# Handing out expert slots after the third, fifth and last group of tokens instead of after every group

## The chip, the cores and the metric

The kernel runs on one core of a Trainium2 chip. The metric is the device time of one execution in microseconds, the median of several runs. A verdict calls a change faster or slower if it moves the time by more than 2%.

## What is computed

A recurrent attention layer is followed by a mixture of experts that sends each token to one expert.

```python
# attention: batch B = 4, heads H = 8, S = 768 steps, head size D = 40, all float32
for t in range(S):
    y[:, :, t] = einsum('bhd,bhde->bhe', r_t, state)
    Sa = einsum('bhde,bhe->bhd', state, a_t)
    state = state * w_t[:, :, None, :] - einsum('bhd,bhe->bhde', Sa, b_t) + einsum('bhd,bhe->bhde', v_t, k_t)
# mixture of experts: N = 3072 tokens of 320, E = 8 experts, F = 1024, capacity N // E * 2
x = y.transpose(0, 2, 1, 3).reshape(B * S, H * D)
logits = x @ w_gate
expert_idx = argmax(logits, axis=1)
gate_w = softmax(logits)[token, expert_idx]
for i in range(N):                       # slots are handed out in the order of the tokens
    e = expert_idx[i]
    if counts[e] < capacity:
        disp[e, counts[e]] = x[i]; pos[i] = counts[e]; counts[e] += 1; keep[i] = True
y = relu(disp @ w1) @ w2
out[i] = gate_w[i] * y[expert_idx[i], pos[i]]        # where keep[i]
```

A token's slot within its expert is the number of earlier tokens that chose the same expert. So slots can be handed out in pieces, if each piece adds the counts of those before it.

## The kernel before

**The scan.** The 768 steps are cut into six groups of 128 (numbers 0 to 5), each group into two chunks of 64. The 32 pairs of batch and head are held in two halves (pr 0 and 1). Within a group the recurrence is solved in a closed form; the state passes from chunk to chunk. For each group there are these steps, told with their lines:

- Decay on VectorE (DVE): products of w by two scans, L378 and L388, with small steps between (L382 to L401, which give the factors wf), and products with them, L458 and L462.
- Matrices on TensorE (PE), L479, one for each half and chunk. ScalarE (ACT) copies them out: X (L66) and the parts of xd and x21 (L61, L503). GpSimd (POOL) masks X (L69).
- The inverse on DVE: a transpose (L578), 62 small elimination operations (L592 and L594 in turn, each needs the one before), two transposes back (L599, L603). Its tiles xd, x21, xu and nu exist once, so that the next group's matrices may overwrite them only when this group is done with them. PE combines the result in blocks of 32 (L623), with copies on ACT between (nt, x, nu; L57, L61).
- The chain, for each half and chunk: decay of the state ST on POOL (L672), products with the state and with X on PE (L693, L697), a copy zv and the sum zs on DVE (L710), a product with the inverse (L721), copies sat and sv, a transpose (L743), copies u, and the new state (L756 on PE, L765 on DVE).
- The output for each half and chunk: qp (L775 on PE, copied and masked, L66, L69 or L72), two products on PE (L791, L794), and y (L805 on DVE). ACT and POOL turn y into an x16 tile in float16 (L57, L856, L857), SyncE (SP) sends it through a DMA transpose (L862) to xT, and PE multiplies that with the gate's weights (L873) to logits, which ACT copies to lg (L878). A group gives four such tiles of 128 tokens, 24 in all.

**Slots.** route, called for each group, has five steps. first (L1110 to L1115, and four additions L1141) finds each token's expert and sums the one-hot rows of the tiles on DVE. count (L1147 to L1149) counts with three matmuls. place (L1155 to L1160) adds the counts of the earlier groups (base) and gives slots. gate (L1120 on ACT, L1121 to L1123 on DVE) gives the weight. Then one scatter for each tile (L1126), an indirect DMA issued by POOL, writes the token's number and weight to the slot's place in one of four tables meta in DRAM (tile number modulo four, so that a scatter waits for the landing of that four tiles before it).

**The experts.** The first 384 slots of experts 0 and 1 can be filled from the first five groups alone in most cases. An early expert uses them while the last group is still under way: it loads slot rows (emm), gathers x rows by POOL, transposes them by DMAs from SP (L944), and multiplies (L960, L1293). It needs the route of group 4. After the scan the experts run one after the other (L1420, L1293), with weights that are scaled on ACT (L1212) and DVE (L1213).

**What sets the order.** The code doesn't state an order within the scan. Each step is given to a list scheduler (Schedule.order) with the engine and the time it is thought to take ("V1.9" is 1.9 us on DVE, "A1.25|V.72" leaves a choice between ACT and DVE), with what it needs, and with which buffers it takes and frees. The scheduler has a clock for each engine and picks, again and again, the step with the lowest score: its start, plus an offset by kind of step and engine (LATER), plus MU times a planned time, minus O_TAIL times the length of what follows it. PRICE weighs the engines where a step may go to several. So a number in these tables can change the order on all engines, and which engine does a copy. The tiles of each kind are counted in BUFS. Each engine then runs its own instructions strictly in that order.

Of the kernel before, what the change touches and what calls it, by code (L numbers as in the profile page):

```python
# [232 lines left out]
def scan_part(ctx, tc, two, w, kb, a, r, vt, v, wg, xd, lg, ident, up, SX, slot2, route, prefetch, fill, early):  # L233
# [23 lines left out]
    LATER = {"R": -5.787, "chain": -0.017, "chain:A": 0.307, "chain:P": -0.014, "chain:V": -0.256,  # L257
             "comb": -0.007, "comb:A": 0.394, "comb:P": 0.904, "decay": 1.569, "decay:V": 0.357,
             "diag": -0.034, "diag:A": 0.978, "early": -2.453, "early:G": 0.469, "early:L": 1.687,
             "early_h": 1.778, "early_h:A": -4.479, "early_h:P": -0.724, "early_h:V": -6.743,  # L260
             "early_o": -0.047, "early_o:A": -0.427, "early_o:G": -3.502, "early_x": -3.485,
             "early_x:G": 0.908, "early_x:S": 3.21, "et": -0.621, "et:A": 1.197, "et:P": 0.131, "fill": 4.274,
             "fill:G": -0.037, "gate": 0.055, "gate:G": -0.339, "gate:P": 0.26, "gate:S": -0.32,
             "gate_store": 2.098, "gate_store:L": -3.063, "inverse": 0.815, "kt": 0.567, "kt:P": -0.305,
             "load_a": 1.14, "load_a:L": -1.165, "load_kb": -0.86, "load_kb:L": -2.23, "load_r": 5.886,
             "load_r:L": 0.968, "load_u": 0.991, "load_u:L": 3.288, "load_vt": 0.808, "load_vt:L": -1.101,
             "load_w": -2.214, "load_w:L": -5.588, "mula": 0.698, "mula:V": 0.924, "mulk": -0.886,
             "mulk:V": 1.741, "out": 0.102, "out:P": -0.049, "out:V": -0.009, "prefetch": 0.015,
             "prefetch:A": 0.642, "prefetch:L": -0.989, "prefetch:V": 1.544, "route": 0.842, "route:A": -14.34,
             "route:G": -3.654, "route:P": 0.544, "route:V": 0.373, "sat": -16.107, "state": -0.132,  # L270
             "state:P": 0.475, "unit": 0.317, "unit:A": -1.263, "xd": -8.639, "xt": -1.178, "xt:A": 0.367,
             "xt:P": -0.155, "xt:V": 0.135}
# [747 lines left out]
def tile_kernel(ctx, tc, w, kb, a, r, vt, v, w_gate, w1, w2, out, capacity):  # L1020
# [109 lines left out]
    def route(i, s_):  # L1130


        tiles = slice(B * i, B * i + B)
# [16 lines left out]

        def place():
            ps = s_["ps"]
            rank = glob.tile([P, B, E], F32, name="rank")
            slot = glob.tile([P, B], F32, name="slot")
            nc.vector.tensor_add(rank, ps[:, 0:B * E].rearrange("p (t e) -> p t e", e=E),  # L1155
                                 base[:, i:i + 1, :].to_broadcast([P, B, E]))
            nc.vector.tensor_add(base[:, i + 1, :], ps[:, B * E:(B + 1) * E], base[:, i, :])
# [3 lines left out]
            if EARLY and i == NI - 2:  # L1161
                nc.vector.tensor_sub(most_a, base[0:1, i + 1, 0:2], ebase[0:1, 0:2])
                nc.vector.tensor_scalar_add(base[:, i + 1, 0:2], ebase[:, 0:2], float(CS - EB))

        return first, count, place, lambda: gate(glob, s_["d"], B, tiles), lambda bi: scatter(B * i + bi)
# [442 lines left out]
```

## Time and profile before

| what | us |
|---|---|
| median of 3 runs (713.77 to 723.05) | 720.71 |
| the profiled execution | 720.66 |
| its span in the profile | 718.7 |
| busy in the span: PE / DVE / ACT / POOL | 532.4 / 450.5 / 348.8 / 282.2 |

The profile is of one execution. Busy times are sums over the whole span; the kernel has a scan, up to about 500 us, and the experts behind it, with different limits, so a stretch is read by itself. In rows of the timeline the first number is the start in us, the second the length in us, then engine, line, operation, output and input, and, in brackets, the idle time of the engine before it with what ended it. "x4" stands for four instructions taken together. In rows of groups a bar parts busy time and mean length in ns from the idle time before.

### The profile page before, as it was taken

The page shows a single profiled execution, that of the slowest core. Times are in us where ns is not written, and L with a number is a line of the kernel's source. Part 1 is how long each engine was busy: PE and PEld are TensorE (multiplying, and loading weights), DVE is VectorE, ACT ScalarE, POOL GpSimd, SP SyncE. Part 2 cuts the span into 40 slices and gives each one's busy share as a digit, 9 for nine tenths or more (in the row PEclk, how much of TensorE's full clock was granted, in tenths as well). Part 3 has the DMA queues.
Part 4 walks back from the last instruction along what each step waited for, and adds up shares of the span by engine and source line. Part 5 has one row for each costly group of instructions (what it writes and reads, how often), then busy time and mean ns, then how long its engine had stood idle before and what let it go on. Part 6 is the DMA issues. An engine that isn't in the chain of part 4 may idle for free. (4 is left out here: it accounts for less than half of the span.)

```text
span 718.7 us, 25037 instructions
## 1 busy us (share of the span) xinstructions
PE 532.4 (74%) x10804; PEld 416.3 (58%) x10804; DVE 450.5 (63%) x871; ACT 348.8 (49%) x751; POOL 282.2 (39%) x380
## 2 busy tenths in 40 slices
PE   1712877768776878587589577585988999999891
PEld 0612766757665767577578476453663655665560
DVE  7999688889688888777748953054433254345120
ACT  4613853675467556654476464334444255245120
POOL 4600454075409541854065325404252153343411
PEclk9965799669857995897579959698998999999996
DMA  8970096917661785276425536746859757856400
GB/s 312 302 231 1 27 206 176 268 46 218 189 214 19 219 218 189 42 201 191 147 52 123 148 105 121 140 104 181 219 103 240 186 110 188 196 152 189 111 20 13
DMA packets 106362, 109.87 MB, mean 153 GB/s; under 512 B 70745, under 2 KB 88667, under 8 KB 106241
## 3 DMA queue, kind: packets, MB, share of 16 engines
q1 hardware_dynamic: 97968, 92.34, 49.1%
q0 software_dynamic: 4256, 9.99, 5.0%
q10 hardware_dynamic: 4016, 5.83, 3.0%
q8 instruction: 87, 1.43, 0.8%
q14 instruction: 35, 0.28, 0.1%
HBM read 83.60 MB, written 10.94 MB: 132 GB/s over the span
## 5 line engine op out<-in xcount | busy, mean ns | idle before, releaser
L1430 DVE SCALAR_TENSOR_TENSOR hh<-ps,hh 128x480 f16<-128x480 f32 (+2 forms) x72 | 37.0, 559 | 107.3 <-ACT hh L1427 107.3
L1293 PE MATMUL ps<-w,hh 128*128 128x320 f16 (+1 forms) x672 | 92.7, 299 | 0.0
L1420 PE MATMUL ps<-xT,w 128*128 128x480 f16 (+1 forms) x448 | 85.4, 354 | 5.9 <-DMA xT<-xt 5.9
L1126 POOL DMA_INDIRECT meta<-mt,sloti x24 | 41.7, 1739 | 114.4 <-DVE se L382 72.9
L1293 PEld LDWEIGHTS <-hh 128*128 128x128 f16 (+1 forms) x696 | 71.1, 103 | 24.3 <-issue 1.6
L594 DVE TENSOR_TENSOR nu<-nu,xd 128x31 f32<-128x31 f32 (+15 forms) x186 | 80.2, 431 | 5.6
L592 DVE TENSOR_TENSOR xd<-xu,nu 128x31 f32<-128x31 f32 (+15 forms) x186 | 79.3, 426 | 5.6
L1420 PEld LDWEIGHTS <-w 128*128 128x128 f16 (+1 forms) x512 | 43.7, 99 | 66.9 <-issue 28.0
L69 POOL TENSOR_SCALAR_AFFINE_SELECT qp<-qp 64x512 f32<-64x512 f32 x86 | 59.7, 694 | 42.2 <-ACT qp L66 30.4
L69 POOL TENSOR_SCALAR_AFFINE_SELECT X<-X 64x512 f32<-64x512 f32 x48 | 45.9, 956 | 65.7 <-ACT X L66 56.9
L1297 POOL DMA_INDIRECT out_dram<-ob,ri x26 | 26.9, 1036 | 106.8 <-ACT ob L1446 33.7
L1213 DVE SCALAR_TENSOR_TENSOR w<-s,w 128x640 f16<-128x640 f32 (+1 forms) x49 | 47.0, 990 | 14.2 <-ACT w L1212 12.8
L1427 ACT ACTIVATE hh<-ps 128x480 f16<-128x480 f32 (+2 forms) x72 | 31.5, 494 | 47.6 <-PE ps L1420 47.6
L623 PE MATMUL ps<-nu,x 32*32 32x32 f32 x768 | 21.7, 236 | 34.5 <-DVE nu L603 29.5
L1212 ACT ACTIVATE w<-s 128x640 f16<-128x640 f32 (+1 forms) x49 | 41.1, 872 | 12.0 <-DMA s<-in_moe_w_dram 11.9
L1446 ACT ACTIVATE ob<-ps,gs 128x320 f32<-128x320 f32 (+1 forms) x26 | 13.7, 526 | 66.3 <-PE ps L1293 52.3
L693 PE MATMUL pd<-u,X 64*64 64x64 f32 (+1 forms) x768 | 37.4, 255 | 10.7 <-ACT xd L503 7.1
L697 PE MATMUL pd<-ST,a 64*64 64x64 f32 x704 | 32.4, 253 | 16.2 <-POOL ST L672 13.3
L775 PE MATMUL pd<-r,sv 64*64 64x64 f32 x1536 | 35.1, 240 | 10.4 <-issue 8.3
L479 PE MATMUL pd<-a,slot 64*64 64x64 f32 x1536 | 34.6, 257 | 9.6 <-ACT xd L503 7.7
L693 PEld LDWEIGHTS pd<-u,X 64*64 64x64 f32 x768 | 33.2, 167 | 14.1 <-ACT xd L503 7.7
L623 PEld LDWEIGHTS ps<-nu,x 32*32 32x32 f32 x768 | 21.1, 151 | 35.0 <-DVE nu L603 26.7
(178 smaller groups left out, 1199.0 us busy)
## 6 DMA issues: line engine op xcount, KB each, us to landing
R<-in_w_dram SPq DMA_DIRECT2D x24, 512.0 KB
slot<-in_kb_dram SPq DMA_DIRECT2D x24, 512.0 KB
sv<-in_vt_dram SPq DMA_DIRECT2D x24, 512.0 KB
s<-in_moe_w_dram SPq DMA_DIRECT2D x14, 512.0 KB
a<-in_a_dram SPq DMA_DIRECT2D x12, 512.0 KB
r<-in_r_dram SPq DMA_DIRECT2D x12, 512.0 KB
s<-in_moe_w_dram SPq DMA_DIRECT2D x15, 320.0 KB
xd<-x SPq DMA_DIRECT2D x24, 192.0 KB
```

The source lines that it names most:

```text
L69: self.nc.gpsimd.affine_select(x, x, pattern=[[0, x.shape[1]], [1, C]], compare_op=ALU.is_gt, fill=0.0, base=0, channel_multiplier=-1)
L592: return (lambda: nc.vector.tensor_mul(tv, xu[:, s + 1:, s:s + 1].to_broadcast([P, n, m]), nu[:, s:s + 1, 0:m].to_broadcast([P, n, m])), l ...
L594: lambda: nc.vector.tensor_add(o, o, tv))
L623: nc.tensor.matmul(pa[o, u * 32:(u + 1) * 32], x21[f, uu, :], (n1 if which == 0 else ntd)[f, uu, :], start=True, stop=True)
L693: nc.tensor.matmul(pz[half(x), 1, into(h)], T["X"][c][f, cols(h, C)], T["u", c][f, x, wide(h)], start=True, stop=True)
L775: nc.tensor.matmul(pp[half(z), h % 2, cols(4 * x + j, C)], T["sv", c][f, x, j, z, :], T["r"][f, x, j, tok], start=True, stop=True)
L1126: nc.gpsimd.indirect_dma_start(out=meta[t % B][:, :], out_offset=bass.IndirectOffsetOnAxis(ap=su[:, t:t + 1], axis=0), in_=mt[:, t, :], in ...
L1212: return (lambda: nc.scalar.activation(h, s(), AF.Copy, scale=SW), lambda: nc.vector.scalar_tensor_tensor(l, s(), SW, h, ALU.mult, ALU.sub ...
L1213: lambda: nc.vector.scalar_tensor_tensor(l, s(), SW, h, ALU.mult, ALU.subtract))
L1293: nc.tensor.matmul(po[:, :DM], h[l], rr[:, f, :], start=(f == 0 and m == 0), stop=(f == NF - 1 and m == 2))
L1420: nc.tensor.matmul(s_["h", f + z][:, :n], l, rr, start=m % 7 == 0 and m < 14, stop=m >= 14)
L1430: nc.vector.scalar_tensor_tensor(s_["hh"][:, 1, f, :n], s_["h", f][:, :n], 0.0, s_["hh"][:, 0, f, :n], ALU.max, ALU.subtract)
```

## The change

Groups 2, 4 and 5 are left as the places where route is called (ROUTES); it then takes all tiles since the last call: twelve, eight and four. The tiles of first, count and place are as wide as that, the additions of the one-hot rows are as many as tiles. The number of scatters is the same, 24. The scheduler's tables are given other numbers, throughout, and x16 has three tiles for four. The experts after the scan are not changed.

```diff
-    MU = 0.00161
-    O_TAIL = 0.0017
+    MU = 0.00681
+    O_TAIL = 0.0047
-    PRICE = {"V": 9.43, "A": 4, "G": 0.56}
+    PRICE = {"V": 7.38, "A": 2.83, "G": 0.54}
-    LATER = {"R": -5.787, "chain": -0.017, "chain:A": 0.307, "chain:P": -0.014, "chain:V": -0.256,
+    LATER = {"R": -0.588, "chain": 0.076, "chain:A": 0.455, "chain:P": 0.075, "chain:V": -0.454, "comb": -0.05,
...
-            "xd": 1, "x21": 1, "xu": 1, "nu": 1, "zs": 3, "S": 2, "qp": 2, "y": 2, "x16": 4, "xT": 2, "leap": 1}
+            "xd": 1, "x21": 1, "xu": 1, "nu": 1, "zs": 3, "S": 2, "qp": 2, "y": 2, "x16": 3, "xT": 2, "leap": 1}
...
+    ROUTES = [x for x in range(NI) if x >= NI - 2 or x % 3 == 2]
     for i in range(NI):
...
+        if i not in ROUTES:
+            continue
+        i0 = max([x + 1 for x in ROUTES if x < i] or [0])
+        nt_ = 4 * (i + 1 - i0)
         PLAN[0] = i * GT + GT
         add = steps("route")
         L_ = {}
-        first, count, place, gates, scatter = route(i, L_)
-        add(first, "V1.9", needs=[("logits", 4 * i + m) for m in range(4)], gives=("one_hot", i))
+        first, count, place, gates, scatter = route(i0, i + 1, L_)
+        add(first, f"V{1.2 + .175 * nt_:.2f}", needs=[("logits", 4 * i0 + m) for m in range(nt_)], gives=("one_hot", i))
         add(lambda f=count, L=L_: (L.update(ps=get("ps")), f()), pe(1), take=["ps"])
         add(lambda f=place, L=L_: (f(), put("ps", L["ps"])), "V.75", free=["ps"])
         add(gates, "A.12 V.5")
-        for bi in range(B):
-            add(lambda bi=bi, f=scatter: f(bi), "G1.04", gives=("route", i) if bi == B - 1 else None)
+        for t in range(nt_):
+            add(lambda t=t, f=scatter: f(t), "G1.04", gives=("route", i) if t == nt_ - 1 else None)
...
-    def route(i, s_):
-        tiles = slice(B * i, B * i + B)
+    def route(i0, i1, s_):
+        tiles = slice(B * i0, B * i1)
+        n = B * (i1 - i0)
...
-            for m in range(B):
+            for m in range(n):
                 nc.vector.tensor_add(acc[:, m + 1, :], acc[:, m, :], oh[:, m, :])
```

Lines below 890 keep their numbers; those behind are six or seven higher in the changed file (L1126 is L1132, L1155 is L1162, L944 is L950).

**What moves.** In these rows an instruction is given by line, operation, output and input; the number behind a name tells tiles of one kind apart. DVE, behind the inverse of group 2, before:

```order
L603 STREAM_TRANSPOSE nu_162<-xu_161 128x1024
L458 TENSOR_TENSOR slot_94<-slot_94,R_179 128x1024 x2
L1110 TENSOR_REDUCE mx<-lg 128x4
L1111 TENSOR_TENSOR d<-lg,mx 128x32
L1112 TENSOR_TENSOR ne<-lg,mx 128x32
L1113 SCALAR_TENSOR_TENSOR ne<-ne,eidx 128x32
L1114 TENSOR_REDUCE ix<-ne 128x4
L1115 TENSOR_TENSOR oh<-eidx,ix 128x32
L1141 TENSOR_TENSOR acc<-acc,oh 128x8 x4
L462 TENSOR_TENSOR a_119<-a_119,R_179 128x1024
L378 SCALAR_TENSOR_TENSOR R_180<-R_180,seed 128x1024
L1155 TENSOR_TENSOR rank<-ps_115,base 128x32
```

and now:

```order
L603 STREAM_TRANSPOSE nu_162<-xu_161 128x1024
L458 TENSOR_TENSOR slot_94<-slot_94,R_178 128x1024 x2
L462 TENSOR_TENSOR a_119<-a_119,R_178 128x1024
L378 SCALAR_TENSOR_TENSOR R_179<-R_179,seed 128x1024
L382 TENSOR_TENSOR se_187<-R_179 128x32
L384 RECIPROCAL leap_177<-se_187 128x16
L385 RECIPROCAL si_189<-se_187 128x16
L388 SCALAR_TENSOR_TENSOR R_179<-R_179,leap_177 128x1024
L393 TENSOR_TENSOR R_179<-R_179,si_189 128x16x32
L398 TENSOR_TENSOR wf<-se_187 128x8
L400 TENSOR_TENSOR wf<-we,se_187 128x8
L401 COPY we<-se_187 128x8
```

The route's instructions (L1110 to L1160 and L1121 to L1123) are gone there, and L388 of the other half follows sooner. They are gone behind the inverse of group 1 in the same way. Behind group 3 now stand the L1116 to L1148 of twelve tiles, and behind group 4, right behind L603, their L1162 to L1167.

DVE again, the beginning of the inverse of group 3, before:

```order
L578 STREAM_TRANSPOSE xu_161<-xd_159 128x1024
L710 TENSOR_TENSOR zs_165<-pd_114,zv_157 128x320
L592 TENSOR_TENSOR xd_159<-xu_161,nu_162 128x31
L594 TENSOR_TENSOR nu_162<-nu_162,xd_159 128x31
L592 TENSOR_TENSOR xd_159<-xu_161,nu_162 128x60
L594 TENSOR_TENSOR nu_162<-nu_162,xd_159 128x30x2
```

and now:

```order
L578 STREAM_TRANSPOSE xu_161<-xd_159 128x1024
L592 TENSOR_TENSOR xd_159<-xu_161,nu_162 128x31
L594 TENSOR_TENSOR nu_162<-nu_162,xd_159 128x31
L592 TENSOR_TENSOR xd_159<-xu_161,nu_162 128x60
L594 TENSOR_TENSOR nu_162<-nu_162,xd_159 128x30x2
L592 TENSOR_TENSOR xd_159<-xu_161,nu_162 128x87
L594 TENSOR_TENSOR nu_162<-nu_162,xd_159 128x29x3
L592 TENSOR_TENSOR xd_159<-xu_161,nu_162 128x112
L594 TENSOR_TENSOR nu_162<-nu_162,xd_159 128x28x4
L765 TENSOR_TENSOR ST_213<-ps_116,ST_212 128x8x40
L710 TENSOR_TENSOR zs_165<-pd_114,zv_157 128x320
```

The sum zs_165 stood directly behind the transpose L578; now eight eliminations stand ahead of it. In the inverse of group 2 it is eleven, in that of group 4 seven.

POOL, behind the inverse of group 4, before:

```order
L1139 MEMSET acc 128x8
L1126 DMA meta_70<-mt,sloti 6144x4
L1126 DMA meta_71<-mt,sloti 6144x4
L1126 DMA meta_72<-mt,sloti 6144x4
L1126 DMA meta_73<-mt,sloti 6144x4
L69 AFFINE_SELECT X_147<-X_147 64x512 x2
L69 AFFINE_SELECT X_148<-X_148 64x512 x2
L672 TENSOR_TENSOR ST_212<-ST_212,wf 128x8x40
L69 AFFINE_SELECT X_149<-X_149 64x512 x2
L69 AFFINE_SELECT X_150<-X_150 64x512 x2
```

and now, with eight further scatters ahead of these rows:

```order
L1132 DMA meta_70<-mt,sloti 6144x4
L1132 DMA meta_71<-mt,sloti 6144x4
L1132 DMA meta_72<-mt,sloti 6144x4
L1132 DMA meta_73<-mt,sloti 6144x4
L69 AFFINE_SELECT X_147<-X_147 64x512 x2
L69 AFFINE_SELECT X_148<-X_148 64x512 x2
L69 AFFINE_SELECT X_149<-X_149 64x512 x2
L69 AFFINE_SELECT X_150<-X_150 64x512 x2
L672 TENSOR_TENSOR ST_211<-ST_211,wf 128x8x40
```

The twelve scatters stand in one piece ahead of the masks of X and of the decay of the state, which stood behind four. Ahead of the masks behind the inverses of groups 1, 2 and 3 no scatter is left. In the tail eight scatters now stand directly ahead of the same decay of the state.

PE, behind the inverse of group 4, before:

```order
L775 MATMUL pd_114<-r_121,sv_123 64x64 x32
L479 MATMUL pd_113<-a_120,slot_95 64x64 x32
L479 MATMUL pd_112<-a_120,slot_95 64x64 x32
L743 MATMUL ps_115<-ident,sat_126 128x128 x4
L693 MATMUL pd_114<-u_130,X_144 64x64
L697 MATMUL pd_114<-ST_212,a_117 64x64
```

and now:

```order
L756 MATMUL ps_115<-u_128,bk_132 40x40 x16
L743 MATMUL ps_116<-ident,sat_126 128x128 x4
L791 MATMUL ps_115<-S_166,r_121 64x80 x2
L794 MATMUL ps_115<-bk_132,qp_168 64x40 x4
L791 MATMUL ps_115<-S_166,r_121 64x80 x2
L794 MATMUL ps_115<-bk_132,qp_168 64x40 x4
```

Before, the products with the state (L697) follow L743 directly, and the output products L791 and L794 come 32 products later. Now the output products come first.

SP, in the last group, before:

```order
L944 DMA_TRANSPOSE R_179<-R_179 128x6x128 x3
L76 DMA leap_178<-in_moe_w_dram 128x2x320
L944 DMA_TRANSPOSE R_180<-R_179 128x6x128 x2
L862 DMA_TRANSPOSE xT_176<-x_0_172 128x6x128
L944 DMA_TRANSPOSE R_180<-R_179 128x6x128
L76 DMA xd<-x_0_172 128x768
L862 DMA_TRANSPOSE xT_177<-x_1_173 128x6x128
L76 DMA xd<-x_1_173 128x768
```

and now:

```order
L76 DMA emm_98<-meta_73 128x3x4
L950 DMA_TRANSPOSE R_178<-R_178 128x6x128 x2
L76 DMA leap_177<-in_moe_w_dram 128x2x320
L950 DMA_TRANSPOSE R_178<-R_178 128x6x128
L862 DMA_TRANSPOSE xT_176<-x_0_172 128x6x128
L950 DMA_TRANSPOSE R_179<-R_178 128x6x128 x3
L76 DMA leap_177<-in_moe_w_dram 128x2x320
L76 DMA xd<-x_2_174 128x768
L862 DMA_TRANSPOSE xT_175<-x_1_173 128x6x128
L76 DMA xd<-x_0_172 128x768
```

The transposes of x tiles (xT) stood behind five of the early expert's six (R); now one stands some rows ahead of these, one behind three of the six and one behind all.

On DVE the whole program has ten more copies of u, two of bk and two of zv, one each of sat and sv, and six more of nt, which ACT had; of the small instructions of route, 42 less.

More of the change, by code (lines that the diff above doesn't have):

```diff
@@ L256, in scan_part @@
     CLOSE = ""
-    LATER = {"R": -5.787, "chain": -0.017, "chain:A": 0.307, "chain:P": -0.014, "chain:V": -0.256,
[L258 to L272, printed above, removed]
@@ new lines, in scan_part @@
+    LATER = {"R": -0.588, "chain": 0.076, "chain:A": 0.455, "chain:P": 0.075, "chain:V": -0.454, "comb": -0.05,
+             "comb:A": 0.376, "comb:P": 0.776, "decay": 1.394, "decay:V": 0.595, "diag": 0.018,
+             "diag:A": 0.967, "early": -3.147, "early:G": 2.17, "early:L": 0.395, "early_h": 0.787,
+             "early_h:A": -1.767, "early_h:P": -0.455, "early_h:V": -5.98, "early_o": 0.64,
+             "early_o:A": -1.484, "early_o:G": 0.352, "early_x": -3.301, "early_x:S": 2.853, "et": -0.682,
+             "et:A": -1.704, "et:L": 0.597, "et:P": 1.583, "fill": 2.501, "fill:G": 1.421, "gate": 0.117,
+             "gate:G": -2.319, "gate:P": 0.288, "gate:S": -0.34, "gate_store": 1.628, "gate_store:L": -1.311,
+             "inverse": 1.043, "inverse:V": -0.187, "kt": -0.184, "kt:A": -0.192, "kt:P": -0.172,
+             "load_a": 0.338, "load_a:L": -0.847, "load_kb": -7.216, "load_kb:L": 3.964, "load_r": 5.054,
+             "load_r:L": 0.106, "load_u": 0.833, "load_u:L": 2.752, "load_vt:L": -2.747, "load_w": -3.211,
+             "load_w:L": -3.857, "mula": 0.636, "mula:V": 0.095, "mulk": -0.984, "mulk:V": 1.591, "out": 0.081,
+             "out:P": -0.054, "out:V": 0.003, "prefetch": 0.027, "prefetch:A": -0.123, "prefetch:L": -1.724,
+             "prefetch:V": 1.859, "route": 1.209, "route:A": -7.618, "route:G": -3.892, "route:P": 0.729,
+             "route:V": -0.166, "sat": -0.173, "sat:A": -4.97, "state": -0.005, "state:A": 0.582,
+             "state:P": 0.509, "unit": -6.993, "unit:A": 2.289, "xd": -6.011, "xt": -2.768, "xt:A": 0.011,
+             "xt:P": 1.568, "xt:V": -0.286}
@@ L1146, in count @@
             oh, acc = (x.rearrange("p t e -> p (t e)") for x in (s_["oh"], s_["acc"]))
-            nc.tensor.matmul(ps[:, 0:B * E], up, oh, start=True, stop=False)
-            nc.tensor.matmul(ps[:, 0:B * E], ones, acc[:, 0:B * E], start=False, stop=True)
-            nc.tensor.matmul(ps[:, B * E:(B + 1) * E], ones, acc[:, B * E:], start=True, stop=True)
+            nc.tensor.matmul(ps[:, 0:n * E], up, oh, start=True, stop=False)
+            nc.tensor.matmul(ps[:, 0:n * E], ones, acc[:, 0:n * E], start=False, stop=True)
+            nc.tensor.matmul(ps[:, n * E:(n + 1) * E], ones, acc[:, n * E:], start=True, stop=True)
         def place():
             ps = s_["ps"]
[L1153 to L1157, printed above, removed]
+            rank = glob.tile([P, n, E], F32, name="rank")
+            slot = glob.tile([P, n], F32, name="slot")
+            nc.vector.tensor_add(rank, ps[:, 0:n * E].rearrange("p (t e) -> p t e", e=E),
+                                 base[:, i0:i0 + 1, :].to_broadcast([P, n, E]))
+            nc.vector.tensor_add(base[:, i1, :], ps[:, n * E:(n + 1) * E], base[:, i0, :])
             nc.vector.tensor_mul(rank, rank, s_["oh"])
@@ L1160, in place @@
             nc.vector.tensor_copy(sloti[:, tiles], slot)
[L1161 to L1165, printed above, removed]
+            if EARLY and i1 == NI - 1:
+                nc.vector.tensor_sub(most_a, base[0:1, i1, 0:2], ebase[0:1, 0:2])
+                nc.vector.tensor_scalar_add(base[:, i1, 0:2], ebase[:, 0:2], float(CS - EB))
+        return first, count, place, lambda: gate(glob, s_["d"], n, tiles), lambda t: scatter(B * i0 + t)
     def route_all(pool, ps):
```

4 lines of the change are left out of this document (2 added, 2 removed).

## The prediction

> **What bounds it now.** I read the table by stretches first, then the waits of DVE and PE, then the timelines of DVE, ACT, POOL and PE in one period. The profiled execution took 720.66 us, its span 718.7 and the 2 us around it; the median of the runs is 720.71, so the sum can be made on either. In the table the columns are the stretch, its length, the busy time of PE, PEld, DVE, ACT and POOL, the clock, the DMA share and GB/s.
>
> ```profile
> 200.00:270.00 70.00, 52.52 (x1594) 48.01 (x1594) 60.08 (x119) 41.95 (x97) 36.20 (x41) 0.79 0.59 164
> 548.00:718.70 170.70, 152.72 (x942) 91.21 (x940) 61.37 (x83) 63.74 (x107) 51.18 (x60) 0.97 0.57 133
> ```
>
> The scan has a period of some 70 us per group, DVE is the busiest (60.08 of 70), and the experts at the end are PE's and stay as they are. What has to be won, is won in the six periods and in the tail between 415 and 500. A period is a loop through single buffers: preparation on DVE and ACT, the transpose L578, 62 eliminations on DVE, L599, L603, and again. The preparation behind the inverse of group 2, on DVE, then ACT:
>
> ```profile
> 201.85 1.25 DVE L603 STREAM_TRANSPOSE nu<-xu 128x1024 f32<-128x1024 f32 x1
> 205.25 0.18 DVE L1110 TENSOR_REDUCE mx<-lg 128x4 f32<-128x32 f32 x1
> 207.23 1.22 DVE L462 TENSOR_TENSOR a<-a,R 128x1024 f32<-128x1024 f32 x1
> 212.10 0.19 DVE L1155 TENSOR_TENSOR rank<-ps,base 128x32 f32<-128x32 f32 x1 [1.46 <-ACT nt L61]
> 213.36 0.19 DVE L382 TENSOR_TENSOR se<-R 128x32 f32<-128x32 f32 x1
> 228.11 0.16 DVE L401 COPY we<-se 128x8 f32<-128x8 f32 x1
> 228.46 1.95 DVE L578 STREAM_TRANSPOSE xu<-xd 128x1024 f32<-128x1024 f32 x1 [0.19 <-ACT xd L503]
> 232.85 0.49 DVE L710 TENSOR_TENSOR zs<-pd,zv 128x320 f32<-128x320 f32 x1 [2.44 <-ACT zv L57]
> ...
> 212.04 0.23 ACT L1120 ACTIVATE d<-d 128x32 f32<-128x32 f32 x1
> 215.01 1.29 ACT L61 ACTIVATE nt<-ps 32x256 f32<-32x256 f32 x4 [0.81 <-PE ps L623]
> 218.41 0.86 ACT L57 COPY u<-ps 64x320 f32<-64x320 f32 x2
> 224.68 0.59 ACT L66 COPY X<-pd 128x512 f32<-128x512 f32 x1 [0.67 <-PE pd L479]
> 227.66 0.76 ACT L503 ACTIVATE xd<-pd 32x256 f32<-32x256 f32 x2
> ```
>
> Two engines end together there: DVE's own preparation at 228.27, ACT's copies at 228.42; L578 waits 0.19 us. So a gain on DVE alone buys nothing; it counts as far as ACT follows. Right behind L578 DVE waits 2.44 us for the copy zv. The cause of that wait lies on POOL:
>
> ```profile
> 213.72 1.01 POOL L1126 DMA_INDIRECT meta<-mt,sloti  x1 [17.16 <-DVE se L382]
> 217.25 3.98 POOL L1126 DMA_INDIRECT meta<-mt,sloti  x1 [0.30 <-issue]
> 224.43 5.07 POOL L69 TENSOR_SCALAR_AFFINE_SELECT X<-X 64x512 f32<-64x512 f32 x4
> 229.58 0.72 POOL L672 TENSOR_TENSOR ST<-ST,wf 128x320 f32<-128x320 f32 x1
> 230.35 0.37 PE L697 MATMUL pd<-ST,a 64*64 64x64 f32 x1 [3.04 <-POOL ST L672]
> ```
>
> The four scatters hold POOL from 213.72 to 224.43, the masks and the decay of the state L672 stand behind them, PE waits 3.04 us for the state, and zv and zs come after it. DVE's waits from 128 to 415 us in sum (us, times, longest) say that it is no single case:
>
> ```profile
> DVE zs L710 <- ACT zv L57: 13.5, 5, 4.0
> DVE rank L1155 <- ACT nt L61: 8.8, 4, 4.3
> ```
>
> **The change, part by part.** *Routes that go, behind the inverses of groups 1 and 2.* On DVE the ten instructions from 205.25 to 207.23 cost 1.98 us, the wait 1.46, the eight from 212.10 to 213.36 another 1.26: 4.7 us off. The new order puts two copies of u there (0.86 by ACT's row) and, behind group 1, two copies of nt, a copy of zv and a zs that stood elsewhere. No row has these copies on DVE; at 0.5 to 0.7 us each, between the 128x320 zs (0.49) and ACT's own 128x512 copy (0.59) with some room, DVE's net is 3.8 us behind group 2 and about 1.7 behind group 1. ACT loses u (0.86), the exponential (0.23), and the waits 0.81 and 0.67, which PE's count matmuls and the late second half of a (L462) stand behind: 2.57. The smaller of the two counts: 2.5 and 1.7, together 4.2. Its ends: 0, if the tail of L623 sets ACT's end anyway, and 2 x 3.8.
>
> *Behind group 3* the first half of the twelve-tile route comes in: six instructions on three times the width and twelve additions for four, while eight instructions and the wait go. Ten cost 1.98, so the eight more additions cost about 1.6 at the same 0.2 us; the wider forms have no row, between 0.18 (no dearer) and 0.54 (three times). That adds 1.6 to 3.7 against 2.7 removed: nothing, and I take nothing.
>
> *The wait behind L578, groups 2, 3, 4.* Without scatters POOL can mask X as ACT delivers it, and L672 no longer comes at 229.58. In the new order zs stands behind seven to eleven eliminations, so that even an unmoved zs would find DVE at work. Of the row's five waits (13.5 us) three stand behind L578; at 2.5 us each, after the one shown, that is 7.5, which I take. The ends are 0 (the wait moves to a later zs or ST) and 13.5.
>
> *Group 4 to 5.* Here before waits most; and here the twelve scatters now stand in one burst.
>
> ```profile
> 345.20 1.25 DVE L603 STREAM_TRANSPOSE nu<-xu 128x1024 f32<-128x1024 f32 x1
> 358.25 0.19 DVE L1155 TENSOR_TENSOR rank<-ps,base 128x32 f32<-128x32 f32 x1 [4.26 <-ACT nt L61]
> 369.45 2.07 POOL L69 TENSOR_SCALAR_AFFINE_SELECT X<-X 64x512 f32<-64x512 f32 x3 [2.37 <-DMA meta<-mt,sloti]
> 378.75 0.49 DVE L805 SCALAR_TENSOR_TENSOR y<-ps,E 128x320 f32<-128x320 f32 x1 [8.19 <-PE ps L794]
> 381.90 0.48 DVE L710 TENSOR_TENSOR zs<-pd,zv 128x320 f32<-128x320 f32 x1
> ...
> L1126 POOL DMA_INDIRECT meta<-mt,sloti x24 | 41.7, 1739 | 114.4 <-DVE se L382 72.9
> ```
>
> The 4.26 us go, since place now stands right behind L603 and its matmuls are long done; and PE has the matmuls of y ahead of the product with the state L697, so that the 8.19 us no longer hang on POOL. This y, which L578 follows, stood 33.6 us behind L603; L578 could stand as behind group 2, 26.6 behind it. What replaces the wait is zs: place ends 1.5 us behind L603, the scatters begin at about 2.2, the landing (2.37) and eight masks (0.69 each, 5.5) and L672 (0.72) follow, and zs 2.7 us behind that. With twelve scatters at a pitch p zs comes at 13.5 + 12p; before it came at 36.7. The quickest pitch of the trace is 1.28 (429.70 to 430.98, below), which gives 28.9 and a gain that L578 limits to 7; the mean, 1.74 and 0.30 between, gives 38.0 and a loss of 1.3. I take the middle, 3 gained.
>
> *The tail.* The route of eight tiles follows the last inverse:
>
> ```profile
> 426.39 1.73 POOL L1126 DMA_INDIRECT meta<-mt,sloti  x1 [19.11 <-DVE mt L1123]
> 429.70 0.97 POOL L1126 DMA_INDIRECT meta<-mt,sloti  x1 [0.31 <-issue]
> 430.98 0.97 POOL L1126 DMA_INDIRECT meta<-mt,sloti  x1 [0.30 <-issue]
> 436.99 0.66 POOL L69 TENSOR_SCALAR_AFFINE_SELECT qp<-qp 64x512 f32<-64x512 f32 x1 [4.36 <-DMA meta<-mt,sloti]
> 437.73 0.72 POOL L672 TENSOR_TENSOR ST<-ST,wf 128x320 f32<-128x320 f32 x1
> 459.75 0.40 PE L873 MATMUL ps<-wg,xT 128*128 128x8 f16 x9 [8.13 <-DMA xT<-x]
> 443.50 7.35 SPq L944 DMA_TRANSPOSE R<-R  x3
> 456.30 1.24 SPq L862 DMA_TRANSPOSE xT<-x  x1
> ```
>
> L672 now follows eight scatters directly, without the masks and their 4.36 us. From 427.5 (1.1 us later than before, for the eight-tile first half by the price above) it comes at 427.5 + 8p: 437.7 at 1.28, as before, and 443.8 at 2.04, a loss of 6. On SP the transposes of the x tiles (L862) now stand ahead of most of the early expert's (L944), which took the queue from 443.50 to 456.30 while PE waited 8.13 us: up to 8 gained. But the early expert's loads hang on the landing of eight scatters instead of four. Between -6 and 8 I take 1 gained.
>
> *At nothing:* the last place on DVE now stands behind casts of weights; its rows are needed 34.8 us after its scatters (below), and PE did not wait between. With three x16 buffers for four, a cast waits for the DMAs of the third tile before it; the tiles come in two pairs a half period apart, and DVE's y would show it first.
>
> ```profile
> 486.99 1.04 POOL L1126 DMA_INDIRECT meta<-mt,sloti  x1 [16.91 <-DVE m L1515]
> 521.74 0.94 PE L1420 MATMUL ps<-xT,slot 128*128 128x128 f16 x14
> ```
>
> Sum: 4.2 + 0 + 7.5 + 3 + 1 = 15.7 us, 720.7 - 15.7 = 705.0.
>
> **The rivals.** *Slower: the bursts.* Four scatters between 213.72 and 224.43 had a pitch of 2.68 us, where DVE was busy all the time; in the tail, with DVE idle, 1.28. At 2.68 zs of group 5 comes at 45.7, 9.0 late, and the tail's L672 at 448.9, 11.2 late; with 4.2 and 7.5 gained the time is 720.7 - 11.7 + 20.2 = 729. The point from which it decides: 20p - 33.4 passes 11.7 at a pitch of 2.26. For it speaks that DVE is dense behind L603 in group 5; against it, that the four scatters which stood there before, beside a DVE that waited at times, took from 359.88 to 366.40, a pitch of 1.6.
>
> ```profile
> 359.88 1.01 POOL L1126 DMA_INDIRECT meta<-mt,sloti  x1 [20.36 <-DVE se L382]
> 365.43 0.97 POOL L1126 DMA_INDIRECT meta<-mt,sloti  x1 [0.31 <-issue]
> ```
>
> The Trainium skill, SBUF — State Buffer, section SBUF: two separate sides, has the rule behind it: while DVE runs an operation in a two-port mode, GpSimd cannot write the descriptors of its DMAs, and a DMA of about 620 ns took about 3100. By that figure twelve scatters would take 40.8 us with the 0.30 between, an estimate, and the time come out near 727 with the tail as before; the trace agrees in kind (0.97 idle, 3.98 at worst). The copies that move to DVE (nt, from SBUF to SBUF) are of the kind it names.
>
> *No change: something else sets the loop.* ACT's end hangs on the tail of L623, and the wait for zv moves to ST (L765), behind PE. Then only half of the 7.5 and nothing of the 4.2 is left, with group 5 and the tail at nothing: 717. The even balance of DVE and ACT speaks for it, PE's 3.04 us for POOL against it.
>
> *The late last route.* If the last scatters come over 10 us later, the rows for the first ordinary expert are late and PE stands for some 6 us: 711. For it speaks the order of DVE, against it the 34.8 us.
>
> *All of it:* both preparations by 3.8, all 13.5 of the zs waits, 3 in group 5, 1 in the tail: 720.7 - 25.1 = 695.6.
>
> **How the numbers follow.** The forecast (698 to 709) has 0.47, no change (713 to 722) 0.20, the late route (709 to 713) 0.08, all of it (690 to 698) 0.12, the bursts (722 to 738) 0.13. The range from 692 to 723 leaves out the bursts and the best of all of it. A measurement of this kernel tells 2% from no change, so the bounds are 706.3 and 735.1: faster has the all and some 0.34 of the forecast, 0.46; slower only the far end of the bursts, 0.06; the rest, 0.48, is the same.
>
> **What would show it.** In the new profile: no scatter before 345; the distance from L603 to L578 some 2 us shorter behind groups 1 and 2; no wait of zs behind L578; PE's wait for the state (L697 before, L703 after) near zero but for group 5; L578 of group 5 some 28 us behind L603 and its zs no more than 37 behind; the pitch of the twelve below 2; the 8.13 us of the tail at most half. Wrong it is made by a pitch over 2.26, by waits of ST that take the place of zs, or by PE standing ahead of 521.

## The result and the profile after

The changed kernel takes 706.66 us in the median of 16 runs (700.38 to 709.84), the kernel before 718.39 (708.89 to 724.07, 16 runs). The ratio that was recorded is 0.9847, with a 95% interval from 0.982 to 0.9875 (the two medians give 0.9837): a gain of 1.5%, too small for the bound of 2%, so the verdict at that bound is "same", but clear of noise. Run once more, beside three other kernels, it was 0.9849 (0.9784 to 0.9914). The forecast was 705.0.

The two profiles differ by more, 718.7 to 699.9 us of span. The run that was profiled took 701.83, 4.8 under its median, and that of before 720.66, 2.3 over the median of all its runs; so some 7 of the 18.8 us are the choice of runs. The table gives, from the timelines, when L603 (the end of a group's inverse) starts, when PE starts the first ordinary matmul of the experts (L1420, after the change L1427), and the span. The last two columns are experiments told below.

| | before | after | after less before, of the stretch | only the tables | only the grouping |
|---|---|---|---|---|---|
| L603, group 0 | 64.7 | 61.2 | -3.5 | 60.7 | 64.5 |
| group 1 | 129.9 | 125.9 | -0.5 | 125.9 | 128.6 |
| group 2 | 201.9 | 193.9 | -4.0 | 196.4 | 199.9 |
| group 3 | 272.1 | 260.5 | -3.6 | 261.0 | 268.1 |
| group 4 | 345.2 | 328.3 | -5.3 | 345.0 | 355.0 |
| group 5 | 416.2 | 402.0 | +2.7 | 431.2 | 420.1 |
| experts | 500.0 | 482.6 | -3.2 | 514.1 | 515.0 |
| span | 718.7 | 699.9 | -1.4 | 738.0 | 737.3 |

Each column is one profile. Six profiles have the order of the changed kernel up to L603 of group 4: the change twice, and e5, m_all, m_from4 and p_g01, told below. From one L603 to the next group 2 takes 68.0 to 72.8 us in them, group 3 65.7 to 66.8, and group 4 66.8 to 70.0. Before it was 71.9, 70.3 and 73.1, and in e3, where every engine has the order of before, 72.5, 69.1 and 71.7. So shorter groups 3 and 4 belong to the change. The 4.0 us of group 2 are not shown to: four of the six take 71.6 or more.

First the waits in the changed kernel from 128 us to the end of the last inverse, for DVE and for PE (us in total, times, longest), and one of PE's rows:

```profile
DVE ST L765 <- PE ps L756: 9.0, 8, 2.6
DVE qp L72 <- PE pd L775: 6.4, 2, 3.6
DVE zs L710 <- ACT zv L57: 3.2, 3, 1.7
DVE xu L578 <- ACT xd L503: 2.7, 2, 1.6
...
PE pd L697 <- POOL ST L672: 4.9, 2, 2.7
...
288.60 0.27 PE L697 MATMUL pd<-ST,a 64*64 64x64 f32 x1 [2.12 <-POOL ST L672]
```

The waits of zs, 13.5 us before, are 3.2. PE's waits for the state (L697 in both kernels), 9.8 us in three times before, are 4.9 in two: 2.1 in group 4, where no scatter stands ahead of it, and 2.7 in group 5. Between the start of L578 and the first elimination there are now 2.0 us in groups 2 and 3 and 1.9 in group 4, the transpose itself, where 4.8, 4.8 and 5.1 were. A wait that was 0.4 us has grown: L578 for ACT. The preparation behind group 2:

```profile
193.91 1.22 DVE L603 STREAM_TRANSPOSE nu<-xu 128x1024 f32<-128x1024 f32 x1
208.85 1.01 DVE L57 COPY u<-ps 64x320 f32<-64x320 f32 x2 [1.05 <-PE ps L743]
217.49 0.49 DVE L765 TENSOR_TENSOR ST<-ps,ST 128x320 f32<-128x320 f32 x1 [2.03 <-PE ps L756]
220.86 2.00 DVE L578 STREAM_TRANSPOSE xu<-xd 128x1024 f32<-128x1024 f32 x1 [1.58 <-ACT xd L503]
```

It still takes 26.9 us from L603 to L578 (26.6 before), without any of route's work: DVE waits instead, in three places, 4.7 us in all, where it had waited 2.2 (the 1.46 of route among them). The last wait is for ACT's copy L503, the end of ACT's own preparation. And the one stretch that became longer, group 5, on POOL, PE and DVE, with POOL's row of the state before at the end:

```profile
331.54 1.32 POOL L1132 DMA_INDIRECT meta<-mt,sloti  x1 [7.23 <-DVE mt L1129]
344.85 0.97 POOL L1132 DMA_INDIRECT meta<-mt,sloti  x1 [4.52 <-DMA meta<-mt,sloti]
354.51 0.97 POOL L1132 DMA_INDIRECT meta<-mt,sloti  x1 [0.30 <-issue]
359.91 4.87 POOL L69 TENSOR_SCALAR_AFFINE_SELECT X<-X 64x512 f32<-64x512 f32 x7 [3.73 <-DMA meta<-mt,sloti]
364.87 0.72 POOL L672 TENSOR_TENSOR ST<-ST,wf 128x320 f32<-128x320 f32 x1
365.64 0.36 PE L697 MATMUL pd<-ST,a 64*64 64x64 f32 x1 [2.73 <-POOL ST L672]
356.50 0.69 DVE L72 TENSOR_TENSOR qp<-pd,mask 128x512 f32<-128x512 f32 x1 [3.56 <-PE pd L775]
361.39 1.99 DVE L578 STREAM_TRANSPOSE xu<-xd 128x1024 f32<-128x1024 f32 x1
368.14 0.49 DVE L710 TENSOR_TENSOR zs<-pd,zv 128x320 f32<-128x320 f32 x1 [1.73 <-ACT zv L57]
...
371.60 0.72 POOL L672 TENSOR_TENSOR ST<-ST,wf 128x320 f32<-128x320 f32 x1
```

The twelve scatters run from 331.54 to 355.48. Two waits for landings, 4.52 us within the burst and 3.73 at the masks, and stretched scatters make the state come 36.6 us behind L603, where it came 26.4 behind before; zs follows at 39.9 (36.7 before). L578 stands at 33.1, for DVE waits for PE's qp products, which PE has behind the matrices L479.

### The profile page after: what moved, and what is told of

It is laid out like the page before. It is cut to its first block, busy times and chain, and to the rows that moved or that the text cites. A ratio compares the mean times of both kernels' runs of the same rounds, so it can differ in the third digit from the quotient of the medians.

```text
span 699.9 us, 24921 instructions
## 1 busy us (share of the span) xinstructions
PE 537.4 (77%) x10786; PEld 415.4 (59%) x10786; DVE 459.4 (66%) x853; ACT 334.3 (48%) x722; POOL 269.8 (39%) x371
## 5 line engine op out<-in xcount | busy, mean ns | idle before, releaser
L69 POOL TENSOR_SCALAR_AFFINE_SELECT X<-X 64x512 f32<-64x512 f32 x48 | 51.4, 1070 | 119.0 <-ACT X L66 113.3
L592 DVE TENSOR_TENSOR xd<-xu,nu 128x31 f32<-128x31 f32 (+15 forms) x186 | 83.3, 448 | 5.7
L1427 PE MATMUL ps<-xT,w 128*128 128x480 f16 (+1 forms) x448 | 82.6, 346 | 2.6 <-DMA xT<-xt 2.5
L1427 PEld LDWEIGHTS <-w 128*128 128x128 f16 (+1 forms) x512 | 42.6, 97 | 53.8 <-issue 16.4
L69 POOL TENSOR_SCALAR_AFFINE_SELECT qp<-qp 64x512 f32<-64x512 f32 x78 | 54.1, 694 | 40.4 <-ACT qp L66 31.0
L1220 DVE SCALAR_TENSOR_TENSOR w<-s,w 128x640 f16<-128x640 f32 (+1 forms) x49 | 47.4, 994 | 11.7 <-ACT w L1219 11.6
L794 PE MATMUL ps<-bk,qp 128*64 128x40 f32 x768 | 41.2, 237 | 12.3 <-POOL qp L69 7.7
L1132 POOL DMA_INDIRECT meta<-mt,sloti x24 | 28.7, 1197 | 56.5 <-DVE mt L1129 43.5
L479 PE MATMUL pd<-a,slot 64*64 64x64 f32 x1536 | 35.5, 258 | 10.2 <-ACT xd L503 5.5
L794 PEld LDWEIGHTS ps<-bk,qp 128*64 128x64 f32 x768 | 36.2, 154 | 11.4 <-POOL qp L69 9.9
L479 PEld LDWEIGHTS pd<-a,slot 64*64 64x64 f32 x1536 | 32.6, 170 | 14.1 <-ACT xd L503 6.8
L856 POOL TENSOR_TENSOR x<-y,x 128x320 f16<-128x320 f32 x24 | 19.9, 830 | 54.2 <-ACT x L57 34.3
```

Of the source, the lines that this page charges most:

```text
L69: self.nc.gpsimd.affine_select(x, x, pattern=[[0, x.shape[1]], [1, C]], compare_op=ALU.is_gt, fill=0.0, base=0, channel_multiplier=-1)
L479: nc.tensor.matmul(pt[half(x if z else 1 - x), z, h * C:(h + 1) * C], kb_, T["a"][half(x), h, tok(c)], start=True, stop=True)
L592: return (lambda: nc.vector.tensor_mul(tv, xu[:, s + 1:, s:s + 1].to_broadcast([P, n, m]), nu[:, s:s + 1, 0:m].to_broadcast([P, n, m])), l ...
L794: nc.tensor.matmul(py[half(x), cols(h)], R["qp"][:, h % 2, 4 * x + j, :], T["bk"][c][:, x, cols(h)], start=q == 0, stop=q == 0 or h % 2 == 1)
L1220: lambda: nc.vector.scalar_tensor_tensor(l, s(), SW, h, ALU.mult, ALU.subtract))
L1427: nc.tensor.matmul(s_["h", f + z][:, :n], l, rr, start=m % 7 == 0 and m < 14, stop=m >= 14)
```

## The experiments

**The two halves of the change.** The grouping without the new tables, the tables without the grouping, and the third x16 tile alone:

```diff
  # e1: the changed kernel with MU, O_TAIL, PRICE and LATER of before (x16 stays at 3)
  # e2: the kernel before with these tables and "x16": 3 of the changed one
  # e3: the kernel before
-            ... "x16": 4, ...
+            ... "x16": 3, ...
```

> The grouping alone: slots behind groups 2, 4 and 5, but the scheduler's tables of before (x16 has three tiles, since four no longer fit beside the wider tiles of route). Theory A (the gain comes from the scatters and route's work that leave the preparations behind the inverses of groups 1 to 3): the time is near the changed kernel's, 704 to 711, and the wait of zs behind L578 is gone in groups 2, 3 and 4, whatever the tables. Theory B (the gain comes from the new order that the tables give): 716 or more, with the waits of zs still there.

> The tables alone: slots behind every group as before, with the new tables and three x16 tiles. Theory A: the scatters still stand ahead of the masks of X, the state still comes late, and the time stays within 714 to 722. Theory B: 704 to 711, since zs stands behind eliminations and the order is that of the changed kernel.

> The kernel before with three x16 tiles instead of four and nothing else. The prediction put this at nothing: within 716 to 722. If the fourth tile was worth something, the cast of the third and fourth tile of a group is late and the time is 722 or more.

The grouping alone is slower than before, 1.0206 (1.0122 to 1.029), and the tables alone too, 1.0268 (1.0182 to 1.0353). Neither theory stands as it was put: both halves lose, and together they win. The third tile costs nothing, 1.0 (0.995 to 1.0051); it pays for the wider tiles of route, beside which a fourth has no room.

The grouping alone does win at first: 4.0 us by the end of group 3, with no scatter in the preparations. But the old tables put the twelve scatters into the inverse of group 4:

```profile
299.91 1.22 POOL L1132 DMA_INDIRECT meta<-mt,sloti  x1 [1.19 <-DVE mt L1129]
309.55 0.97 POOL L1132 DMA_INDIRECT meta<-mt,sloti  x1 [2.50 <-DMA meta<-mt,sloti]
314.83 1.01 POOL L1132 DMA_INDIRECT meta<-mt,sloti  x1 [4.32 <-DMA meta<-mt,sloti]
325.80 0.97 POOL L1132 DMA_INDIRECT meta<-mt,sloti  x1 [4.38 <-DMA R<-in_w_dram]
328.86 0.72 POOL L672 TENSOR_TENSOR ST<-ST,wf 128x320 f32<-128x320 f32 x1
329.63 0.36 PE L697 MATMUL pd<-ST,a 64*64 64x64 f32 x1 [9.47 <-POOL ST L672]
```

POOL needs 26.9 us for them, a decay of the state stands behind, and PE waits 9.47 us; that period is 86.9 us long, after 68.1. What is left is lost behind the last inverse (95.0 us to the experts, 83.8 before). The tables alone give the gain of group 0 and follow the changed kernel to group 3. Then the preparations behind groups 3 and 4 take 42.1 and 50.3 us from L603 to L578. Behind group 4 DVE has two routes there, with copies and sums that stood elsewhere, and waits in seven places, 14.6 us in sum; the longest, and L578:

```profile
353.86 0.19 DVE L1155 TENSOR_TENSOR rank<-ps,base 128x32 f32<-128x32 f32 x1 [2.40 <-ACT nt L61]
363.04 1.19 DVE L1141 TENSOR_TENSOR acc<-acc,oh 128x8 f32<-128x8 f32 x4 [2.40 <-POOL acc L1139]
372.50 0.49 DVE L710 TENSOR_TENSOR zs<-pd,zv 128x320 f32<-128x320 f32 x1 [3.87 <-ACT zv L57]
395.29 1.97 DVE L578 STREAM_TRANSPOSE xu<-xd 128x1024 f32<-128x1024 f32 x1
```

The sum zs, which in the changed kernel stands behind eliminations, here stands ahead of L578.

**What made zs wait: scatters left out, order kept.** Empty steps take the scheduler's place of the scatters, so that each engine's order is that of before.

```diff
-            add(lambda bi=bi, f=scatter: f(bi), "G1.04", gives=...)
+            add((lambda: None) if i < 3 else lambda bi=bi, f=scatter: f(bi), "G1.04", gives=...)
```

> The kernel before without the scatters of groups 0, 1 and 2; all else in the same order. Their tokens get no slot, so only the scan is to be compared. The prediction's step: the scatters on POOL make the state (L672) late, and that is the wait of zs behind L578. Then PE's wait for the state falls from 3.0 to 3.7 us to under 0.7 and DVE's wait from 2.4 to 2.7 to under 1 in groups 2, 3 and 4, and L603 of group 4 comes 5 to 7.5 us earlier. The rival, that the place of zs directly behind L578 makes the wait (zv cannot be there yet): the wait stays over 1.5 us in each group and L603 of group 4 moves by less than 3.

The ratio is 0.9841 (0.9761 to 0.9921), with half of the tokens without a slot. Waits from 128 to 345 us in sum, for PE and DVE before, then for DVE without these scatters:

```profile
PE pd L697 <- POOL ST L672: 9.8, 3, 3.7
DVE ST L765 <- PE ps L756: 7.9, 8, 2.2
...
DVE ST L765 <- PE ps L756: 11.5, 8, 3.8
DVE zs L710 <- ACT zv L57: 4.1, 3, 1.8
```

PE's wait for the state, 9.8 us in three times over the same stretch before, is at most 0.4 in each group, and zs, still directly behind L578, waits no longer there: the first elimination comes 2.3 us behind the start of L578 in all three groups, for 4.8, 4.8 and 5.1. So the scatters made that wait, as the prediction had it, and the place of zs did not. But of these 7.9 us only 2.3 are left at L603 of group 4, counted from that of group 1 (213.0 us for 215.3), and in e3, whose engines have the order of before, that distance is 213.3; so even the 2.3 lie within what two profiles of one order differ by. Part of the rest is a wait of DVE for ST, 11.5 for 7.9; the remainder can't be told from the differences between two profiles. So the expectation of 5 to 7.5 us failed, and so did its rival, which had the wait stay.

**Route's work left out, order kept.**

```diff
         first, count, place, gates, scatter = route(i, L_)
+        if i < 2:
+            first = count = place = gates = lambda: None
+            scatter = lambda bi: None
...
+    nc.gpsimd.tensor_copy(base[:, 2, :], ebase)
```

> The kernel before without any of route's work for groups 0 and 1 (L1110 to L1126); all else in the same order. Their tokens get no slot, so only the scan is to be compared. The prediction's step, that route's work on DVE and PE costs 1.5 to 2.5 us of each preparation: L603 to L578 goes from 26.8 and 26.6 to about 25 behind groups 1 and 2, and with the waits of zs in groups 2 and 3 gone L603 of group 3 comes 7 to 9 us earlier. The rival, that ACT's copies set the end of the preparation: L603 to L578 stays above 26, and only the 5 us of the waits are gained.

From L603 to L578 it still takes 26.9 and 26.6 us behind groups 1 and 2; before it took 26.8 and 26.6. The rival holds. By group 3 L603 comes 5.6 us earlier than before, counted from group 1 (4.9 earlier than in e3), about the two waits of zs. The whole is 0.9743 (0.967 to 0.9816), with a third of the tokens without a slot. On DVE and ACT behind group 2:

```profile
216.93 0.49 DVE L765 TENSOR_TENSOR ST<-ps,ST 128x320 f32<-128x320 f32 x1 [4.96 <-PE ps L756]
224.70 1.97 DVE L578 STREAM_TRANSPOSE xu<-xd 128x1024 f32<-128x1024 f32 x1
...
211.07 1.29 ACT L61 ACTIVATE nt<-ps 32x256 f32<-32x256 f32 x4 [0.82 <-PE ps L623]
220.71 0.59 ACT L66 COPY X<-pd 128x512 f32<-128x512 f32 x1 [0.67 <-PE pd L479]
223.69 0.76 ACT L503 ACTIVATE xd<-pd 32x256 f32<-32x256 f32 x2
```

On DVE the 4.7 us of route became a wait of 4.96 us (0.58 before) for the new state, which stands there in DVE's order; ACT's waits, 0.82 and 0.67, are as before, so route had not caused them.

**The burst in group 5.** The changed kernel without its twelve scatters, order kept as above.

> The changed kernel without the twelve scatters behind the inverse of group 4; every other instruction stands in the same order. Their tokens get no slot, so the experts have fewer rows; only the scan is to be compared. The theory that the burst holds the state (L672) and with it zs of group 5: zs comes 4 to 8 us earlier, the inverse of group 5 from first elimination to L603 goes from 38.4 to about 34, and the scan's end comes 4 to 6 us earlier. The rival, that PE's own order (the qp products behind the matrices, L775 and L479) sets the length of that group: L578 stays 33 behind L603 and less than 2 us are gained.

The ratio is 0.9726 (0.9641 to 0.9812), with half of the tokens without a slot. Group 5 (L603 to L603) takes 66.8 us instead of 73.7. L578 stands 30.8 behind L603 instead of 33.1, and from the first elimination on the inverse takes 33.7 instead of 38.4:

```profile
363.24 0.72 POOL L672 TENSOR_TENSOR ST<-ST,wf 128x320 f32<-128x320 f32 x1 [1.67 <-DVE ST L765]
365.38 1.98 DVE L578 STREAM_TRANSPOSE xu<-xd 128x1024 f32<-128x1024 f32 x1
369.03 0.48 DVE L710 TENSOR_TENSOR zs<-pd,zv 128x320 f32<-128x320 f32 x1
```

The state now comes 28.7 us behind L603, and zs 34.5, 5.4 earlier. L578 is not free even so: DVE still waits 3.03 us for PE's qp products ahead of it. So PE's order, the rival, holds L578 back in part, but more was gained than the 2 us that it left room for. The burst costs 6.9 us here, and 5.3 against the second profile of the change, in which group 5 takes 72.1. On which side of L578 the burst costs this is not settled. In the first profile 4.7 of the 6.9 lie behind L578. In the second all of it lies ahead: L578 stands 36.4 behind L603, and from the first elimination on the inverse takes 33.4, no longer than without the burst. Two rows of the second:

```profile
359.40 0.69 DVE L72 TENSOR_TENSOR qp<-pd,mask 128x512 f32<-128x512 f32 x1 [5.80 <-PE pd L775]
363.50 2.01 DVE L578 STREAM_TRANSPOSE xu<-xd 128x1024 f32<-128x1024 f32 x1
```

**Other places for the burst, and other groupings.** In the changed kernel all twelve scatters, or the last eight, had to wait in the scheduler for the matrices of group 5; or the offset of the scatters was changed; or slots were given out elsewhere.

```diff
-            add(lambda t=t, f=scatter: f(t), "G1.04", gives=...)
+            add(lambda t=t, f=scatter: f(t), "G1.04", needs=[("X", 2 * NI - 1, c) for c in range(2)]
+                if i == 2 and t == 0 else [], gives=...)        # m_all; m_from4: t == 4
-             "route:G": -3.892
+             "route:G": 0.1                                      # p_g01
-    ROUTES = [x for x in range(NI) if x >= NI - 2 or x % 3 == 2]
+    ROUTES = [1, 3, 4, 5]                                       # g_r1345; g_r345: [3, 4, 5]
```

> The changed kernel with the twelve scatters made to wait, in the scheduler, for the masks of X of group 5, so that they stand behind these masks on POOL; the decay of the state that stood behind them then goes to DVE. The theory that the burst holds group 5: the scan's end 3 to 6 us earlier and the time 701 to 704. The rival, that the burst only fills a gap: 705 to 708, since the early expert's rows and the later scatters give it back.

> The changed kernel with only the last eight of the twelve scatters made to wait for the masks of X of group 5: four scatters, masks, eight scatters. If the burst's cost is the number of scatters ahead of the masks and the state, the first masks come some 8 us earlier, zs of group 5 no more than 37 behind L603, and the ratio is 0.975 to 0.982. If the eight scatters behind only move the wait to the qp masks, as in the kernel with all twelve behind, it is 0.985 to 0.992.

> The changed kernel with one number of the table different (route:G 0.1 for -3.892): nine scatters ahead of the masks of X, three singly behind; in the tail the decay of the state stands ahead of the eight scatters. If the tail is held by the state, the ratio falls to 0.975 to 0.984; if it is held by the early expert's rows, which then come some 8 us later, it rises to 0.988 or more.

> The changed kernel's tables, with slots behind groups 1, 3, 4 and 5, for eight, eight, four and four tiles: two bursts of eight and one of four in place of one of twelve and one of eight. If the long bursts cost what theory A takes from the trace (the landing of a scatter four places ahead, 4.5 us, and the masks behind), the time is 702 to 706. If scatters between the masks cost more than their number, as behind groups 1 to 3 before, it is 707 to 712.

> The changed kernel's tables with slots behind groups 3, 4 and 5, for sixteen, four and four tiles. By the number of scatters alone a burst of sixteen instead of twelve costs 4 x 1.3 to 2 us more in group 5 and the tail wins as much by four instead of eight: 0.98 to 0.99. If the tables fit only the grouping that they were made for, as the grouping behind 1, 3, 4 and 5 says, it is slower than the kernel before: 1.0 to 1.03.

> The changed kernel once more, beside the next three on the same chip: 0.982 to 0.988 of the kernel before. Its spread between profiles is what is to be seen: the inverse of group 2 (38 to 46 us in kernels with the same order up to there) moves the end by some 5 us either way.

| | ratio to before | 95% interval | L603 of group 4 to group 5, us | L603 of group 5 to the experts, us |
|---|---|---|---|---|
| the change, once more | 0.9849 | 0.9784 to 0.9914 | 72.1 | 79.4 |
| m_all | 0.9877 | 0.9812 to 0.9942 | 82.5 | 82.3 |
| m_from4 | 0.9814 | 0.9748 to 0.9881 | 77.8 | 83.3 |
| p_g01 | 0.9832 | 0.9753 to 0.991 | 68.8 | 94.3 |
| g_r1345 | 1.0284 | 1.02 to 1.0369 | 87.8 | 80.7 |
| g_r345 | 1.0191 | 1.0119 to 1.0264 | 90.7 | 80.3 |

No place of the burst is told from the change by its time; the lowest ratio, 0.9814, lies within the interval of the change in the same set of runs. With all scatters behind the masks zs of group 5 comes no earlier, and a y waits 6.09 us for PE. With the offset changed group 5 wins 3.3 us against the change in the same set of runs, and the tail loses 14.9 up to the experts, though the last product with the gate's weights (L873) stands 2.0 earlier behind L603. The early expert's rows come late, and PE waits for them:

```profile
469.97 0.80 PE L966 MATMUL pd<-R,slot 128*128 128x384 f16 x2 [6.34 <-DMA R<-R]
```

So there the tail hangs on these rows. What an earlier state would give in the tail this run can't say, since its last decay of the state stands 28.2 us behind L603, in the change of the same set 25.9. The two other groupings with the same tables are slower than the kernel before. Their profiles show the same long preparations as the tables alone: 50.2 and 56.6 us, or 42.7 and 58.4, from L603 to L578 behind groups 3 and 4.

Of these expectations two came out: the change once more lies within its range, and g_r345 is slower, as tables made for one grouping would have it. m_all has group 5 longer, not shorter. m_from4 has the lower ratio that its first theory asked for, but zs of group 5 at 39.4 us for no more than 37. p_g01 has a ratio of the range for a tail held by the state, and a tail that waits for the rows: there the number fits and the mechanism does not. g_r1345 lies far above both of its ranges.

## Why the prediction was right, and where not

The time was right by 1.7 us, and part of that was luck. The gain was forecast at 15.7 us and measured at 11.7; the kernel before had been taken at 720.7 and has a median of 718.4 over 16 runs, which hides 2.3 of the difference. And the sum has terms that were right and others that made up for them.

- **The wait behind L578** (7.5 us): right that it goes, and that the scatters were its cause. The three first eliminations are 2.8, 2.8 and 3.1 us nearer to L578, some 0.5 of each for the zs that stands later now. What that is worth is not shown. That the wait moves on to ST, the lower end of that step, is right in part too: in the kernel before without scatters at most 2.3 us were left. In the changed kernel the stretches of groups 2, 3 and 4 are 4.0, 3.6 and 5.3 us shorter, of which the first may be the profile's.
- **The preparations** (1.7 and 2.5 us): the sizes came out at 1.5 and -0.3, and the reason was wrong. The step failed where ACT's waits of 0.81 and 0.67 were put down to route, and where DVE and ACT were taken for all that ends there: a DVE with less work waits for the state and for ACT, whose wait of 0.81 stands in the changed kernel too. The rival of no change had this, that ACT's end stays. What made it 1.5 us shorter behind group 1 was not tried by itself.
- **Behind group 3** (nothing): right, 26.0 for 26.4.
- **Group 5** (3 us gained): wrong in sign, 2.7 lost (1.1 in the second profile). The step failed where the pitch was set between rows that hold no wait of a scatter for an earlier one's landing. With the usual 0.30 us in place of that wait of 4.52 the pitch is 1.64 and zs comes at 33.2, 3.5 earlier than before, near what was taken; with it the pitch is 2.0, which by the sum gives 37.5. zs came at 39.9, past the worse end of 38.0, since the scatters began 3.3 us behind L603 for 2.2 and the landing ahead of the masks took 3.73 us for 2.37. And L578 was not free to stand at 26.6: four copies of qp (L72) stand on DVE ahead of it, two before, and their products came late from PE; without the burst it stood at 30.8. The rival of the bursts, scatters stretched beside a busy DVE, had a part of it at a smaller size: they took 4.7 us more than 0.97 each, and 7.6 in the second profile, where the burst took as long with waits of 2.20 (no releaser shown) and 0.94 us between scatters.
- **The tail** (1 us gained): 3.3. Before and after, PE's waits behind the last inverse:

```profile
PE ps L873 <- DMA xT<-x: 10.2, 2, 8.1
PE ps L1420 <- ACT zs L1313: 7.7, 1, 7.7
...
PE ps L873 <- DMA xT<-x: 1.6, 2, 1.1
PE ps L1427 <- ACT zs L1320: 0.6, 1, 0.6
PE ps L794 <- POOL qp L69: 5.9, 4, 2.1
```

  The wait for xT fell as forecast. The decay of the state behind the eight scatters came 22.7 us behind L603 (21.5 before), within the bounds, and the last one, on DVE now, 25.8. The wait of the experts for zs was not in the sum at all, and neither was what took much of both gains back: PE's waits for POOL's masks of qp (5.9 us for 0.3), and 4.6 us more of busy PE.
- **Group 0**, 3.5 us, was not in the sum either. With the tables alone it is 4.0, with the grouping alone 0.2: the tables did it, by an order that the text left out.
- **The late last route and no change:** neither came. PE stood 0.6 us at the start of the experts.
- **The unspoken step:** the text took the grouping for the cause, with the tables as its means. The runs show that either half alone loses. No run has tables made anew for the old grouping, so how much of the gain the grouping itself gives is open.

What remains open besides is how the 7.9 us that vanish behind L578 without scatters were given back in the kernel before, of which only the wait for ST was seen, and so which waits make up the 11.7 us of the change.

## What to carry to other kernels

Work taken off an engine pays only as far as the next instruction in its order is ready; look for what that instruction waits for before the freed time is counted. The scatters here write the same few tables and wait for each other's landings; a burst of twelve met such a wait (4.52 us) where four at a time had met none between them. And where a planner's tables set the order, tables and structure are one thing: judge a new structure with tables made for it, and expect tables to lose on another structure.

## What the hardware showed unexpectedly

With the same order of instructions on all engines up to there, the inverse of group 1 took 36.9, 35.9 and 36.0 us in three profiles (the change twice, p_g01) and 39.1, 39.0 and 39.0 in three others (e5, m_all, m_from4). The stretch from 87 to 126 us in the change, the change once more, and e5:

```profile
87.00:126.00 39.00, 29.60 (x790) 26.19 (x790) 36.38 (x75) 19.20 (x46) 18.94 (x29) 0.87 0.78 205
87.00:126.00 39.00, 26.97 (x798) 24.04 (x800) 37.03 (x76) 19.54 (x47) 18.42 (x29) 0.95 0.76 207
87.00:126.00 39.00, 32.65 (x788) 29.14 (x788) 33.79 (x74) 17.68 (x43) 17.47 (x27) 0.76 0.74 202
```

In these rows PE has the same matmuls and is busy 27.0 to 32.7 us for them, at granted clocks from 0.95 to 0.76. In the three faster profiles the clock was 0.87, 0.95 and 0.95, in the three slower 0.76, 0.82 and 0.84. In the three slower ones DVE waits 2.8 to 3.0 us once in this stretch for the new state (L763), in the others not. That the clock made this wait is not shown. In the inverse of group 2 the same six took 40.7 to 45.6 us. So differences of 3 to 5 us in a stretch between single profiles of this kernel are not the kernel's.

And scatters of 128 rows took 0.97 us with DVE idle, but up to 3.99 while DVE ran three TENSOR_TENSORs of 128x1024 (L458 twice and L462, in the kernel before). Not every operation of that size does it: at 337.23 us in the change one took 0.97 beside a scan of 128x1024. A wait for landings stopped POOL for 4.52 us in the burst, and for up to 6.82 (p_g01, ahead of the masks of qp).

The Trainium skill, SBUF — State Buffer, section SBUF: two separate sides, tells of such slow DMAs from GpSimd as of a lock that DVE's two-port modes take. The runs show the size, not which of DVE's operations held the port.
